# Gated linear attention with a soft mixture of experts on one core: products in the q,k tile, one guard on ScalarE, 8 KB weight places, stores from two engines, and a new order of issue

## The chip, the cores and the metric

The kernel runs on 1 core of one Trainium2 chip. The metric is device time in microseconds (us), the median of several runs; before the change it is 292.26 us (3 runs, 291.92 to 292.39). All data are float32. Engines go by the profile's names: PE is TensorE (PEld its weight loads), DVE VectorE, ACT ScalarE, POOL GpSimd, SP SyncE, whose queue here issues the DMAs.

## The reference

A gated linear recurrence with a complex state is computed for 4 batches x 8 heads, 768 steps, head dimension 48; its outputs are the tokens (3072 x 384) of a soft mixture of 8 experts with 4 slots each.

```python
mag = np.sqrt(a_re * a_re + a_im * a_im)
scale = np.minimum(mag, 0.999) / (mag + 1e-06)
a_re_n, a_im_n = (a_re * scale, a_im * scale)
for t in range(S):
    ar, ai = (a_re_n[:, :, t, :, None], a_im_n[:, :, t, :, None])
    new_re = ar * S_re - ai * S_im
    new_im = ar * S_im + ai * S_re
    kv = np.einsum('bhd,bhe->bhde', k[:, :, t], v[:, :, t])
    S_re, S_im = (new_re + kv, new_im)
    y[:, :, t] = np.einsum('bhd,bhde->bhe', q[:, :, t], S_re)
...
logits = x @ phi
d = softmax of logits over the tokens;  slot_input = d.T @ x
for e in range(E):
    h = np.maximum(slot_input[e] @ w1[e], 0.0)
    slot_out[e] = h @ w2[e]
c = softmax of logits over the slots;   return c @ slot_out
```

## The kernel before, in words

**Tiles.** The 768 steps of a batch are cut into 6 blocks of 128, 24 blocks g in all; three blocks make a unit u (8 units), whose gates, q and k, and v are loaded in one DMA each (tiles `aat`, `qkt`, `vt`, two buffers each). The weights of the experts are cut into chunks in the order in which they are used, 12 chunks of w1 with 8 KB and 11 of w2 with up to 9 KB in each partition. 17 of the 23 fit into places that are free before the experts begin: 7 in the pool `wx`, 4 in the last buffers of `aat` and `qkt`, 4 in `we`, 2 in `wt`. The other 6 reuse `wx` once the hidden layer has read what lies there.

**Steps.** All work is written as small generators, one for each task; a task's name is a letter and a number, and each time that its name stands in the string `ORDER` its next step is issued. `_InOrder` then pins the order on every engine: what stands first in `ORDER` runs first on its engine, and different engines meet only by their semaphores. SP's DMAs are pinned among themselves too, so one that waits holds back those behind it. The steps which matter here:

- `g` (gates, a group of blocks; group 0 is the first block alone, group 1 the rest of unit 0, group 2 is unit 1): a guard (L647 on DVE for the groups below `GUARD_V`, L650 on ACT for the others), then logarithm and exponential on ACT (L652, L654), two steps of DVE (L656, L658), ACT L660, DVE L662, ACT L664, DVE L666. `t` takes the arctangents (L682).
- `e` (exponentials of a block): PE sums the logarithms (`lp`, L724), ACT makes two exponentials into `ee` (L731, L733), and a DMA takes one row of them to `rows` (L736). `d` loads these rows back as the decay of the state (`rt`, L740).
- `p` (phase): DVE carries the phase from the block before (L690), PE sums (`up`, L693), DVE or ACT rounds (L697, L699), DVE L702, ACT the sine (L707), DVE L710, ACT the cosine (L712).
- `m` (products): DVE multiplies q and k by the exponentials, in place in `ee` (L747), then expands the result by sine and cosine into `hat` (L752).
- `x` transposes (PE L764, copy by DVE L768 or ACT L770), `c` scores (PE L775, mask on DVE L779), `a` attends (PE L800 and L802, ACT L805), `D` updates the state (PE L813, DVE L818, L820), `f` turns the output (PE L825).
- `l`, `q`, `s`, `me`, `si` are the router, its running softmax and the merge into the slots' inputs; `er` makes the tokens' weights (PE L290); `H`, `R`, `U`, `X` are the experts (hidden layer L241, then L271, 128 output columns in each of three X), `O` the slots' outputs (L282, L284), `A` combines (PE L300, evicted by ACT L306 or DVE L308) and `S` stores (L981, four stores for each X).
- `wu` are 19 products of a tile of zeros (`blank`, L928) between the first steps of PE; `w` load weights; `i`, `la`, `lq`, `lv` load the inputs; `rp` loads two constant matrices; `L` and `T` load ACT's tables.

The in-place product is the reason why a DMA stands among the computing engines: L747 writes `ee`, from which the row transfer L736 reads, so it waits for that transfer to land.

Of the kernel before, what the change touches and what calls it, by code (L numbers as in the profile page):

```python
# [95 lines left out]
class _Moe:  # L96
# [220 lines left out]
    p4 p4 x6 g3 g3 e4 e4 e4 D1 p4 e4 x8 x10 c3 g3 x8 a0 D1 D2 x10 p5 p5 c4 p5 g3 g3 la2 T2 p3 p3 D1 p3 D2 p5 p5 c3 a1 a1 a1 c5
    m3 c4 p4 p4 p4 D2 D2 c5 wu10 t3 a2 p5 p5 m3 a2 g3 x14 a2 L3 m4 p6 x12 p6 e5 m5 x13 p6 l0 l0 f2 D3 g4 x13 x14 f2 p7 p7 x12 m5
    p7 p7 g4 x15 e6 x15 e6 e6 D3 e8 e8 e8 p8 d1 c6 m4 c6 e6 l0 D3 q0 q0 g4 f0 f0 x19 x17 x17 g4 g4 x19 p8 q0 x16 x16 e7 e7 e7 s0
    c7 c7 x21 x21 g4 m6 x18 x18 f1 f1 a3 tr0 g4 p8 p8 a3 a3 g4 x20 x20 T3 D3 p6 p6 lq2 e7 la3 q0 lv1 c8 c8 c9 D4 D4 g4 x23 p6 s0  # L320
    s0 x22 x22 c10 p8 p8 a4 c9 a4 t4 x23 m6 x27 p8 p9 p7 p7 D4 p7 c10 c11 D4 c11 L4 m7 p9 p9 p9 a4 m7 x25 e8 x25 x24 x24 p10 g5
    rp0 D5 D5 x27 e9 e9 e9 d2 g5 q0 q0 a5 a5 D5 e9 x26 x26 e10 m8 m8 c12 s0 c12 x31 rp1 g5 x28 x31 q0 x28 c13 e10 e10 g5 g5 a5
    p10 p10 p10 x35 w0 c13 x30 x30 l1 g5 l1 x35 x32 p11 e11 e11 e11 x29 x29 x32 g5 g5 q1 q1 q1 a6 a6 e10 a6 m10 f4 f4 c15 p11
    p11 x34 c15 T4 x34 g5 g5 p9 p9 p9 q1 p11 p11 c14 c14 D6 t5 i5 D6 D6 D6 x33 x33 f3 f3 s0 s0 p11 a7 lv2 p11 a7 p10 q1 q1 a7 D7
    m9 p10 D7 m9 D7 e11 m11 p12 c16 p12 p10 p12 l1 c17 c17 D8 x37 x39 D8 la4 g6 c16 a8 a8 m10 L5 x37 g6 d3 lq3 g6 x39 x36 x36 q1
    x41 x41 x38 g5 e13 x40 e13 e13 x38 D7 D8 lv3 c18 x40 e12 e12 a8 D9 e12 e12 g6 s1 x43 x43 p13 g6 e13 m11 g6 c19 c18 c19 g6
    x42 x42 D8 p13 p13 p13 w1 e14 e14 p14 e14 m12 e14 D9 x45 x45 g6 c20 a9 a9 T5 a9 c20 f5 c21 f5 c21 x44 x44 D9 x47 p12 p12 p12
    g6 p14 p14 p14 x47 la5 x46 x46 p13 p13 f7 f7 p14 p14 t6 l2 l2 a10 lq4 a10 m12 c23 s1 g6 p13 D10 f6 f6 p14 p15 p15 s1 p15 c23
    g6 q2 x50 q2 p15 d4 x50 x51 x51 p15 D10 D9 a10 p15 p15 p16 L6 c22 e15 c22 c25 x48 x48 p16 p16 a11 a11 m13 x49 m13 D10 D11
    D11 x53 g7 p16 e15 c25 e15 p17 x49 e16 m14 m14 c24 q2 c24 a11 s1 e17 g7 e16 e16 D11 g7 g7 e17 e17 x55 x55 x53 s1 s1 a12 a12  # L330
    x54 x54 p17 p17 e15 e16 l2 s2 g7 x52 x52 p17 m15 q2 g7 g7 x57 x57 D12 x56 x58 x58 l3 x56 l3 c27 a12 lv4 x59 x59 c27 l3 g7 s2
    s2 c26 q2 f10 D11 q2 w2 f8 w3 c28 c26 a13 a13 T6 t7 f8 p18 m15 f10 p16 p16 p16 D12 p17 p17 q2 f9 p17 g7 p18 c28 x63 f9 s2
    x63 x61 x61 x62 x62 D12 D13 p18 p19 la6 q3 D13 a13 p18 x60 x60 p19 p19 c29 p18 m16 c30 p18 q3 m16 p19 e17 g7 c29 g8 p19 lq5
    L7 x67 q3 a14 a14 s2 x67 f11 f11 d5 a14 lv5 g7 e18 D12 D13 D14 x65 D14 e18 e18 g8 g8 s2 c30 m17 m17 c31 e19 e19 e19 x64 x65
    x64 D13 x68 x68 a15 c31 a15 lq6 s3 x69 e20 e20 x69 g8 e20 g8 p19 g8 x66 x66 p20 e18 m18 s3 s3 m18 c32 c32 x71 T7 s3 p20 D14
    l4 a15 f12 p20 t8 p19 c33 c33 f12 e19 c34 e20 p20 x71 a16 a16 q3 p20 p20 q3 p20 c34 D15 g8 x70 x72 m19 q3 x70 x73 d6 c35 D14
    D15 x72 l4 q4 c35 q3 m19 D15 x73 c36 s3 L8 s3 a16 g8 a17 a17 a17 x76 g8 g8 x78 x78 c36 p21 q4 D16 q4 x75 x75 f13 w4 x76 g8
    l5 w5 l5 e23 e23 x74 D16 x74 x77 f13 m20 m20 x77 p21 p21 p21 e23 c37 x79 e22 e22 e22 c37 x80 q4 x80 e21 e21 e21 f15 e21 x79
    l4 D16 p22 f14 f14 q4 q4 f15 D16 q4 a18 a18 q5 c38 q5 x83 c38 x81 a18 s4 s4 s4 f16 lv6 q5 T8 s4 x83 m21 p22 p22 c39 c39 a19
    a19 x81 p22 p23 p22 p21 p21 e22 p21 m21 s4 s4 p23 p23 p23 f16 x82 x82 p23 p23 D17 D17 D17 D17 c40 c40 x84 c41 c41 x86 D18  # L340
# [4 lines left out]
    er1 w9 w12 ze0 si0 er3 er2 si0 w11 H0 H0 H0 H0 H0 H0 H0 G0 H0 H0 R0 H0 w10 w13 w14 H0 er1 w15 w16 q7 q7 q7 er2 U0 U0 H0 U0
    X0 X0 X0 X0 X0 R1 q7 U1 er7 er7 U1 X0 X0 X0 X0 U1 X0 X0 X0 X0 X0 X0 G0 G0 X0 X1 w17 w18 X1 X1 X1 X1 X1 O0 O0 A3 A4 A5 A5 A2
    A2 A3 X1 X1 X1 A4 S1 S3 X1 X1 X1 X1 A0 A0 er8 A1 er6 X1 X1 X1 X2 X2 A1 X2 X2 X2 X2 O1 er8 O1 S0 er6 A6 A6 S2 A13 A13 A8 A8
    X2 A12 A7 A12 S6 A10 X2 X2 X2 X2 G0 G0 G0 A7 S4 X2 X2 X2 X2 A10 X2 O2 O2 A9 A9 S5 G0 A11 A14 A11 A15 A15 A14 S8 A17 A16 A16
# [197 lines left out]
def _polar(ctx, tc, cst, phi_sb, rp, bad, aa, qk, vv, phi, w1, w2, consts, out):  # L546
# [79 lines left out]
    def wload(pool, **kw):  # L626
# [5 lines left out]
        if x < NW1:  # L632
            SP.dma_start(out=t[:, 0 : W1C * F_], in_=w1[x])
        else:
            c = W2C if x < NW1 + NW2 - 1 else W2L
            SP.dma_start(out=t[:, 0:c], in_=w2[x - NW1][:, 0:c])
# [479 lines left out]
```

## Time and profile before

| what | value |
|---|---|
| runs | 292.39, 291.92, 292.26 us |
| profiled execution | 291.88 us, span 290.1 us |
| granted clock of TensorE, mean | 0.978 |
| busy: PE, PEld | 270.6, 216.3 us |
| busy: DVE, ACT, POOL | 233.2, 218.2, 5.0 us |
| DMA | 54.84 MB, 189 GB/s in the mean |

The span is from the first to the last instruction; the rest of the execution's own time lies around it. A busy time is the time in which the engine executes; a matmul's end is modelled, so a busy PE may also be waiting. Each row of a view by windows gives, for a stretch of the span, the busy time of each engine (with the number of instructions), the clock granted to TensorE as a share of full speed, the share of time in which the DMA engines move data, and GB/s. A row of the chain of waits gives the start, the length, and what was on the chain that ended last. A row of a timeline gives start, length, engine, line, operation, output and inputs, and in brackets how long the engine had been idle and what ended that.

### The profile page before, as it was taken

The page shows a single profiled execution, that of the slowest core. Times are in us where ns is not written, and L with a number is a line of the kernel's source. Part 1 is how long each engine was busy: PE and PEld are TensorE (multiplying, and loading weights), DVE is VectorE, ACT ScalarE, POOL GpSimd, SP SyncE. Part 2 cuts the span into 40 slices and gives each one's busy share as a digit, 9 for nine tenths or more (in the row PEclk, how much of TensorE's full clock was granted, in tenths as well). Part 3 has the DMA queues.
Part 4 walks back from the last instruction along what each step waited for, and adds up shares of the span by engine and source line. Part 5 has one row for each costly group of instructions (what it writes and reads, how often), then busy time and mean ns, then how long its engine had stood idle before and what let it go on. Part 6 is the DMA issues. An engine that isn't in the chain of part 4 may idle for free.

```text
span 290.1 us, 6872 instructions
## 1 busy us (share of the span) xinstructions
PE 270.6 (93%) x2825; PEld 216.3 (75%) x2825; DVE 233.2 (80%) x424; ACT 218.2 (75%) x394; POOL 5.0 (2%) x11
## 2 busy tenths in 40 slices
...
GB/s 251 364 181 2 165 104 27 309 6 29 344 37 21 215 241 90 84 127 336 15 71 397 234 98 150 85 209 2 80 17 384 365 421 422 105 418 419 235 315 186
DMA packets 20054, 54.84 MB, mean 189 GB/s; under 512 B 11632, under 2 KB 12336, under 8 KB 15408
## 3 DMA queue, kind: packets, MB, share of 16 engines
...
## 4 chain that ended last, share of the span: by engine, by line
PE 80%; DMA 6%; DVE 5%; ACT 4%; issue 1%; SPq 1%; ACTq 0%; DVEq 0%
PE sp L775 14%; PE tp L764 14%; PE db L813 8%; PE yb L800 8%; PE yb L802 6%; PE up L693 4%; DMA rows<-ee 4%; PE op L271 4%; PE xp L825 4%; PE hp L241 4%; PE lp L724 3%; PE lg L118 3%; PE sip L185 2%; DMA aat<-in_aa_dram 2%; PE wp L928 1%; PE o L300 1%
## 5 line engine op out<-in xcount | busy, mean ns | idle before, releaser
L764 PE MATMUL tp<-cst,hat 128*96 128x128 f32 x384 | 53.9, 275 | 3.5 <-DVE hat L752 3.4
L770 ACT COPY hT<-tp 96x512 f32<-96x512 f32 x92 | 51.2, 589 | 6.5 <-PE tp L764 4.3
L764 PEld LDWEIGHTS tp<-cst,hat 128*96 128x96 f32 x384 | 42.3, 128 | 12.2 <-issue 8.1
L775 PE MATMUL sp<-hT,hT 96*128 96x128 f32 x384 | 50.5, 277 | 0.0
L775 PEld LDWEIGHTS sp<-hT,hT 96*128 96x128 f32 x384 | 47.3, 192 | 3.5 <-issue 0.6
L752 DVE TENSOR_TENSOR hat<-ee,cs 128x1536 f32<-128x1536 f32 x24 | 42.0, 1752 | 1.2 <-ACT cs L712 0.7
L800 PE MATMUL yb<-scT,vt 128*48 128x128 f32 x384 | 36.2, 276 | 0.0
L779 DVE TENSOR_TENSOR scT<-sp,cst 128x512 f32<-128x512 f32 x48 | 32.6, 684 | 3.6 <-PE sp L775 3.4
L813 PEld LDWEIGHTS db<-vt,hat 128*96 128x96 f32 x320 | 30.8, 165 | 1.8 <-issue 0.9
L802 PE MATMUL yb<-hT,st 96*48 96x128 f32 x320 | 31.2, 272 | 0.0
L813 PE MATMUL db<-vt,hat 128*96 128x48 f32 x320 | 31.2, 244 | 0.0
L800 PEld LDWEIGHTS yb<-scT,vt 128*48 128x48 f32 x384 | 21.1, 122 | 6.2 <-issue 2.6
L747 DVE TENSOR_TENSOR ee<-ee,qkt 128x768 f32<-128x768 f32 x24 | 22.6, 950 | 2.5 <-DMA rows<-ee 2.4
L928 PE MATMUL wp<-blank 128*128 128x512 f32 x38 | 21.9, 708 | 1.0 <-POOL blank L923 1.0
L693 PE MATMUL up<-aat,cst 128*128 128x384 f32 x48 | 20.1, 500 | 0.0
L802 PEld LDWEIGHTS yb<-hT,st 96*48 96x48 f32 x320 | 19.2, 123 | 0.0
L805 ACT COPY yT<-yb 128x512 f32<-128x512 f32 x24 | 14.3, 594 | 5.7 <-PE yb L802 5.7
L712 ACT ACTIVATE cs<-n,kb 128x384 f32<-128x384 f32 x24 | 14.7, 612 | 2.0 <-DVE n L710 2.0
L731 ACT ACTIVATE ee<-lp 128x384 f32<-128x384 f32 x24 | 12.1, 505 | 5.2 <-PE lp L724 3.6
L928 PEld LDWEIGHTS wp<-blank 128*128 128x128 f32 x38 | 8.6, 238 | 9.3 <-issue 6.5
L724 PE MATMUL lp<-aat,cst 128*128 128x384 f32 x24 | 11.0, 541 | 4.4 <-DVE aat L666 4.4
L707 ACT ACTIVATE cs<-f 128x384 f32<-128x384 f32 x24 | 12.5, 525 | 2.6 <-DVE f L702 2.5
...
## 6 DMA issues: line engine op xcount, KB each, us to landing
...
```

Source lines behind the costliest of these rows:

```text
L693: PE.matmul(out=up, lhsT=tri_u[par], rhs=ph, start=True, stop=True)
L724: PE.matmul(out=lp, lhsT=mask[par], rhs=aat[u][:, j, 0], start=True, stop=True)
L747: DVE.tensor_tensor(out=e, in0=e, in1=qkt[u][:, j], op=ALU.mult)
L752: DVE.tensor_tensor(out=x, in0=e.rearrange("p w (h d) -> p w h d", d=D).unsqueeze(3).broadcast_to(sh), in1=cs[g].unsqueeze(1).broadcast_to ...
L764: PE.transpose(out=tp[:, a, :], in_=hat[g][w][:, 4 * hh + a].rearrange("p c d -> p (c d)"), identity=ident)
L770: ACT.copy(out=hT[g, hh, w], in_=tp)
L775: PE.matmul(out=sp[:, a, :], lhsT=hT[g, hh, 1][:, a, :], rhs=hT[g, hh, 0][:, a, :], start=True, stop=True)
L779: DVE.tensor_tensor(out=t, in0=sp, in1=mask[g % 2].unsqueeze(1).broadcast_to([P, 4, P]), op=ALU.mult)
L800: PE.matmul(out=o, lhsT=vt[u][:, j, h, :], rhs=scT[g, hh][:, a, :], start=True, stop=first)
L802: PE.matmul(out=o, lhsT=st[g - 1][:, h, :], rhs=hT[g, hh, 0][:, a, :], start=False, stop=True)
L813: PE.matmul(out=db[:, h, :], lhsT=hat[g][1][:, h].rearrange("p c d -> p (c d)"), rhs=vt[u][:, j, h, :], start=True, stop=True)
L928: PE.matmul(out=wp.rearrange("p (a c) -> p a c", a=4), lhsT=blank, rhs=blank.unsqueeze(1).broadcast_to([P, 4, P]), start=True, stop=True)
```

## The change

- `mults` writes the products of q, k and the exponentials into the q,k tile and no longer into `ee`; the expansion reads them there.
- `GUARD_V` goes from 3 to 2: the guard of group 2 (unit 1) is done by ACT (L650) and no longer by DVE (L647).
- The places of weights are 8 KB (`W2C` 2048 where it was 2304), w2 has 12 chunks, and `wx` has 8 places, `we` 5: 19 of 24 chunks have a place ahead and 5 reuse `wx`. The output tiles keep their width under a name of its own (`OSC`).
- The row transfer of the first block, and every second store, are issued by ACT.
- `blank` lies in a buffer of `xs`, which it gives back.
- `ORDER` is new in all its lines.

```diff
-W1C, W2C = 2, 2304
+W1C, W2C = 2, 2048
+OSC = 2304
...
-NW1, NW2 = 12, 11
-W2L = 64 * HD - (NW2 - 1) * W2C
-BUF = dict(wx=7, wt=2, f=3, cs=4, ee=3, hat=2, hT0=4, hT1=3, scT=2, st=2, xs=5, yT=5, we=4)
+NW1, NW2 = 12, 12
+BUF = dict(wx=8, wt=2, f=3, cs=4, ee=3, hat=2, hT0=4, hT1=3, scT=2, st=2, xs=5, yT=5, we=5)
...
-SPLIT, GUARD_V, ROUND_V, COPY_V = 4, 3, 4, 1
+SPLIT, GUARD_V, ROUND_V, COPY_V = 4, 2, 4, 1
...
-        SP.dma_start(out=rows[u][:, j, :]...)
+        (SP if g else ACT).dma_start(out=rows[u][:, j, :]...)
...
-        e = ee[g]
-        DVE.tensor_tensor(out=e, in0=e, in1=qkt[u][:, j], op=ALU.mult)
+        qk = qkt[u][:, j]
+        DVE.tensor_tensor(out=qk, in0=ee[g], in1=qk, op=ALU.mult)
...
-            in0=e.rearrange("p w (h d) -> p w h d", d=D).unsqueeze(3).broadcast_to(sh),
+            in0=qk.rearrange("p w (h d) -> p w h d", d=D).unsqueeze(3).broadcast_to(sh),
...
-    blank = cp.tile([P, P], F32, name="blank")
+    blank = ys.tile([P, HD], F32, name="xs", bufs=BUF["xs"])[:, 0:P]
...
-        SP.dma_start(out=stored(out, x, s), in_=os_at(x, *STORES[s]))
+        (ACT if s % 2 else SP).dma_start(out=stored(out, x, s), in_=os_at(x, *STORES[s]))
```

Of the order, the head (to about the first score), some places of the middle, and the end of the merge and of the stores, before and after; steps left out stand as "...":

```diff
-    wu2 i0 g0 wu3 wu18 L0 g0 g0 i2 g0 g0 g0 i4 i3 g1 g0 g0 g1 g0 wu16 wu4 g1 g1 i1 e0 wu15 e0 e0 i6 T0 t0 lq0 g1 t1 wu6 p0 wu5
-    p0 p0 wu13 p0 i7 p0 p0 L1 e0 m0 wu9 g1 m0 x3 g1 wu8 g1 p1 x3 wu14 g1 e1 la0 e1 rp1 g2 g2 g2 x2 x2 e1 e1 p1 p1 wu7 x0 e2 e2
-    e2 p1 p2 g2 g2 g2 m1 x0 p2 T1 p1 wu0 x1 wu12 t2 D0 x1 p2 wu17 p1 wu11 p2 la1 p1 p2 e2 d0 wu1 g2 rp0 c0 lv0 p2 p3 m1 D0 p2 m2
-    L2 c1 x5 g2 g2 x4 x4 x5 c0 p3 p3 g3 g3 e5 ...
+    wu6 wu4 wu1 L0 wu12 wu18 i0 g0 g0 g0 g0 g0 wu17 i3 g0 g0 wu5 g0 i4 g1 g1 g1 rp1 i1 g0 e0 e0 e0 wu3 wu9 T0 t0 g1 g1 t1 e0 i2
+    m0 p0 p0 p0 p0 p0 p0 L1 p1 g1 p1 m0 g1 i7 g1 wu16 i6 wu2 p1 p1 g1 p2 rp0 D0 x2 x2 p2 p2 x3 x3 p2 la0 g2 g2 g2 g2 g2 e1 e1 e1
+    wu0 x1 x1 e2 e2 e2 x0 g2 T1 p1 wu14 lv0 wu10 p2 t2 D0 x0 c0 g2 c0 la1 p1 p1 p2 p2 wu15 m1 a0 p3 wu7 L2 m1 c1 c1 p3 p3 g2 g2
+    x4 x4 a0 a0 x5 x5 wu13 m2 p3 e1 e2 g3 e3 ...
...
-    ... la5 x46 x46 p13 p13 f7 f7 p14 p14 t6 l2 l2 a10 lq4 a10 m12 c23 s1 g6 ... x53 g7
+    ... p14 t6 x46 x46 g6 p12 p12 D9 ... f7 l2 a10 a10 a10 m12 w2 f6 f6 c22 c22 p15 q2 p15 x47 x47 p14 p14 la5 g7
...
-    q7 f20 q7 f20 w7 w8 f23 er0 me0 er0 s6 me0 s6 f21 f21 f22 me0 s7 er4 me0 s7 s7 er3 me0 me0 me0 me0 f22 s7 s7 er5 er5 q7 er4
-    er1 w9 w12 ze0 si0 er3 er2 si0 w11 H0 H0 ...
+    f20 f20 q7 f23 f23 q7 s7 me0 me0 s6 s6 f22 i5 s6 f21 s7 s7 f22 s7 er1 me0 f21 s7 me0 me0 me0 me0 er0 s7 ze0 q7 q7 w13 w12
+    w11 er4 me0 er1 si0 si0 H0 H0 ... U0 er2 er2 U1 w14 er8 U1 er6 ... X0 er5 er3 ... er7 er3 ...
...
-    X2 A12 A7 A12 S6 A10 ... X2 O2 O2 A9 A9 S5 G0 A11 A14 A11 A15 A15 A14 S8 A17 A16 A16
-    A18 A18 A19 A17 S9 A19 A20 S11 A20 S10 S7
+    ... X2 S4 X2 X2 S5 O2 O2 A13 A13 A12 A14 A15 A12 S6 A14 A18 A15 S8 G0 A18 A11 A11 S7 A16
+    A16 A19 A19 S11 A17 A17 S9 A20 A20 S10
```

More of the change, by code (lines that the diff above doesn't have):

```diff
@@ L317 @@
[L317 to L340, printed above, removed]
@@ L345 @@
[L345 to L348, printed above, removed]
@@ new lines @@
+    g3 g3 x7 g3 x7 D1 p4 D1 p5 e4 lq0 g3 x8 x8 wu11 m3 p5 e4 e4 p5 p5 D2 c3 g3 D2 c5 c3 T2 e3 rp1 t3 p3 p3 p3 a1 a1 p6 D1 la2 p5
+    p5 g3 e6 c5 p4 p5 p4 c4 m3 x12 lq1 x13 e4 D2 c4 a1 p6 m4 D3 D3 a2 p6 a2 m5 p7 p4 m4 x12 x13 D2 c6 x14 g4 c6 L3 a2 D3 l0 l0
+    l0 g4 w0 e5 e6 g4 g4 e6 x14 x16 x16 x19 x19 D4 e8 x18 e8 e8 x15 x15 p7 x18 p7 g4 g4 x17 a3 x17 m5 s0 p7 p8 e7 f0 f0 g4 q0 q0
+    e6 e7 e7 d1 D3 g4 f2 f2 c7 c7 c8 c8 p8 la3 q0 q0 s0 T3 p8 x20 lv1 m6 t4 lq2 p8 p7 a3 p7 p7 a3 x21 D4 p6 p6 c9 p8 x23 p9 e7
@@ new lines @@
+    s0 c9 p9 p6 x20 q0 a4 a4 x21 tr0 g4 m6 q0 x23 x22 x22 q0 rp0 p8 p9 c10 w1 c10 p8 D4 x27 x27 a4 g5 L4 x26 x26 s0 x25 x25 e8
+    g5 c11 x24 x24 p9 D5 D5 g5 e9 m8 e9 e9 c11 e10 e10 d2 D4 a5 a5 m7 f1 f1 e10 lv2 m7 x31 x31 x28 x28 c13 m8 p10 p10 g5 g5 p10
+    a5 c12 x30 p10 x29 c12 g5 e11 x29 l1 a6 x30 c13 p11 l1 a6 g5 e11 e11 m11 c14 lq3 D5 q1 q1 x34 a6 g5 c14 x34 p11 p11 m9 q1 q1
+    c15 c15 T4 t5 f3 x33 p9 p10 la4 f3 D6 D6 x35 x35 p11 s0 p9 p9 D6 D6 p12 l1 p11 p11 x32 p10 s0 m9 x32 f4 f4 g5 p11 p10 a7 a7
@@ new lines @@
+    p15 g6 x50 x50 p15 p15 p15 e14 D10 D10 lq4 d4 x51 p16 D10 c23 c23 L6 w3 x48 x51 q2 x49 m13 e15 e15 e15 x48 e15 g7 m14 m14
+    a11 a11 c25 c25 p16 D11 p16 p16 D11 g7 g7 x49 p17 e16 e16 e16 x55 x57 x55 a11 e17 g7 e17 c24 e17 D11 c24 x57 l2 x54 x54 x56
+    D11 p17 p17 l3 p17 g7 g7 q2 q2 l3 x52 x52 s1 x53 a12 a12 x53 x56 s1 lv4 c27 c27 la6 s1 s2 c26 c26 m15 g7 x58 x59 f8 c28 a12
+    e16 a13 a13 T6 p17 p17 t7 x59 p18 p16 D12 g7 p17 p16 x58 c29 p18 a13 w4 m15 q2 D12 p16 f8 m17 x61 w5 p18 s2 c29 g8 c28 p19
@@ L478, in chunk @@
             t = wk.tile([P, W2C], F32, name="sw", bufs=6)
-            n = W1C * F_ if w is w1 else W2C if x < NW2 - 1 else W2L
-            ACT.dma_start(out=t[:, 0:n], in_=w[x][:, 0:n])
+            ACT.dma_start(out=t, in_=w[x])
             chunk.n += 1
```

36 lines of the change are left out of this document (24 added, 12 removed).

## The prediction

> **What bounds the kernel now.** I read the busy time by stretch first, with the cuts at places of the chain, then the chain of waits, then timelines of the first 20 us and the last 12.
>
> ```profile
> 19.49:41.20 21.71, 18.36 (x82) 11.15 (x82) 20.55 (x27) 15.27 (x21) 0.95 (x1) 0.92 0.40 114
> 41.20:60.00 18.80, 18.75 (x183) 15.76 (x184) 18.37 (x28) 18.68 (x31) 0.77 (x2) 1.00 0.48 137
> 60.00:180.00 120.00, 120.00 (x1258) 105.71 (x1257) 115.83 (x185) 118.70 (x216) 0.00 (x0) 1.00 0.52 151
> 180.00:250.00 70.00, 69.51 (x765) 59.74 (x762) 55.76 (x123) 46.64 (x97) 2.03 (x3) 1.00 0.57 214
> 250.00:278.30 28.30, 27.26 (x511) 17.01 (x511) 11.20 (x38) 5.53 (x12) 0.49 (x1) 1.00 0.77 307
> 278.30:290.10 11.80, 2.74 (x9) 1.30 (x9) 2.66 (x5) 2.82 (x6) 0.00 (x0) 0.75 0.62 243
> ```
>
> Columns: stretch, length, busy time of PE, PE's weight loads, DVE, ACT, POOL, granted clock, DMA share, GB/s. From 19.49 to 41.20 DVE works 20.55 of 21.71 us and ACT only 15.27: DVE bounds the head. From 41 to 180 all three are full (ACT 118.70 of 120). After 180 ACT and DVE have room and PE runs on; after 250 it is nearly alone. So what the head saves can reach the end, if the middle doesn't eat it.
>
> ```profile
> 8.12 0.96 DVE gt L647 x2
> 9.08 0.59 DVE aat L662
> ...
> 10.95 1.57 PE lp L724 x2
> ...
> 13.06 5.29 DMA rows<-ee
> 18.42 0.97 DVE ee L747
> ...
> 39.79 1.37 DVE aat L666
> 41.20 0.91 PE lp L724 x2
> 42.12 0.89 PE sp L775 x8
> 43.01 1.01 PE yb L800 x16
> ```
>
> This is the chain (start, length, what). Three places matter. At 8.12 DVE does the guard of the second gate group, after waiting for its load, before the first block's L662. At 13.06 the one-row transfer out of `ee` goes out, lands 5.29 us later, and only then the in-place product L747 starts. At 39.79 the gates of unit 1 are done, and PE gets the sums that it waited for; from here on it has no gap to speak of.
>
> **The head, step by step.** ACT's rows:
>
> ```profile
> 7.06 0.61 ACT L660 ACTIVATE gt<-gt,kb 128x384 f32<-128x384 f32 x1 [1.23 <-DVE tmax L658]
> ...
> 10.21 0.83 ACT L652 ACTIVATE aat<-aat 128x768 f32<-128x768 f32 x1
> 11.07 0.84 ACT L654 ACTIVATE gt<-aat 128x768 f32<-128x768 f32 x1
> ...
> 13.43 1.28 ACT L584 ACT_TABLE_LOAD   x1
> 14.73 1.25 ACT L682 ACTIVATE aat<-aat 128x384 f32<-128x384 f32 x2
> 17.43 0.52 ACT L707 ACTIVATE cs<-f 128x384 f32<-128x384 f32 x1 [1.45 <-DVE f L702]
> 17.86 0.60 ACT L712 ACTIVATE cs<-n,kb 128x384 f32<-128x384 f32 x1
> ```
>
> (a) The new order puts L662 ahead of the guard. It can start when L660 ends, 7.67, and ends at about 8.3; the guard then runs to 9.3 (its data no longer lies behind a q,k piece in the queue), L666, of L662's length, to 9.9, where the matmul starts: 1.0 us earlier than 10.95. ACT puts the second group's logarithm and exponential (0.83 and 0.84) between 9.3 and 11.0, beside the matmul's 1.57, then the two exponentials of L731 and L733, which here took the 0.9 us from the matmul's end at 12.52 to the table load at 13.43; I get 12.0 for their end, 13.3 for the arctangents against 14.73. From the arctangents to the sine it took 2.70 us (PE, then DVE twice), so the sine starts at 16.0 and the cosine ends at 17.1.
>
> (b) The products go into the q,k tile, so L747 waits for no row to land. It now stands before the rounding, at about 13.1, under the phase matmul. The expansion L752 then waits for the cosine alone: 17.1 against 19.49, with which the first stretch above begins: 2.4 us earlier. The row transfer is issued by ACT behind the arctangents, and holds ACT less than the 1.45 us for which it waited there anyway; if it holds it longer than that, the sine is late by the rest.
>
> (c) From that expansion to the end of unit 1's gates DVE decides. The list of its steps in both orders differs by this: the guard of unit 1 and one product leave (the product comes later), two masked scores enter.
>
> ```profile
> 24.44 1.35 DVE L647 TENSOR_SCALAR_CACHE_REDUCE gt<-aat 128x1152 f32<-128x1152 f32 x1
> ```
>
> ```profile
> L779 DVE TENSOR_TENSOR scT<-sp,cst 128x512 f32<-128x512 f32 x48 | 32.6, 684 | 3.6 <-PE sp L775 3.4
> ...
> L290 PE MATMUL ep<-ecT,rp 96*128 96x512 f32 (+2 forms) x18 | 4.5, 351 | 0.0
> ```
>
> That is -1.35 - 0.97 + 2 x 0.68 = -1.0 us of work. Against it I count 0.5 us of waits that were not there (mostly DVE waiting for the logarithm while ACT does the guard that it took over: 1.25 us, if it runs at L652's pace, 0.83 for two thirds of the width). So the gates of unit 1 end 2.4 + 1.0 - 0.5 = 2.9 us earlier. What DVE and ACT have left at that point is the same to 0.5 us in both orders, and PE has done the first block's attention more, which here comes after 41.20 (L800, 1.01). Bounds: 1.5 (ACT's guard on the path in full) to 3.9 (PE's 1.0 carried as well). I take 2.9, the number of DVE, which bounds this stretch.
>
> **The middle.** The rest of the order is mixed anew, but steps of PE stand, all along, behind nearly the same sums of DVE's and ACT's work as before; I price that at nothing, with 2 us either way. ACT covers it: if its 118.70 of 120 rises, there is nothing to take it up until 180.
>
> ```profile
> DVE ee L747 <- DMA rows<-ee: 2.4, 3, 1.1
> ...
> PE op L271 <- issue: 1.0, 1, 1.0
> ...
> PE lg L118 <- DVE d L176: 0.5, 1, 0.5
> ```
>
> These rows (waiting engine, what for; us, times, longest) show three waits of L747 on a row, 2.4 us of DVE; the head's is one, so two of at most 1.1 lie elsewhere. I see one of them reach PE, as the 0.5 us before L118. With the product in the other tile they are gone: 0.5 us, between 0 and 2.2. In exchange the q,k tile comes free an expansion later, so the next load of q,k and what stands behind it on SP's queue (the row transfers, the decay loads, and the state scaling that waits for these) could be late. In the new order each such load stands well behind the expansion that frees it, so I take nothing.
>
> **The tail.** The weights:
>
> ```profile
> 254.00:270.00 16.00, 15.11 (x288) 9.17 (x280) 4.94 (x12) 3.48 (x8) 0.00 (x0) 1.00 1.00 414
> ```
>
> From 254 to 270 all DMA engines move the last six chunks, 414 GB/s x 16 us = 6.6 MB, and PE's wait of 1.0 us above, with no other releaser, lies at the end of that. With 8 KB places 19 of 24 chunks fit ahead instead of 17 of 23, and five are left, 5 x 1.05 = 5.2 MB, 12.7 us: the 1.0 us goes. But three wide weight tiles (L290: nine in 4.5 us, so 0.5 each) move from before the hidden layer to after it, where PE has no gap; ahead of it they filled a wait of the merge, which gets shorter by part of that. I take 0.5 us for both together, between -0.5 and 1.5.
>
> ```profile
> 268.80 16.41 SPq L981 DMA_DIRECT2D out_dram<-os  x12
> ```
>
> ```profile
> 281.99 3.22 SPq L981 DMA_DIRECT2D out_dram<-os  x3
> ```
>
> The twelve stores are issued by SP one behind the other, and the last three alone take 3.22 us, of the 11.80 after the last expert product. With two issuers none stands behind another for so long, but ACT issues three between its last evictions, which at 3.22/3 can delay one of them by up to 1.1 us each. I take 0.5 us, from -1.0 to 1.5. The Trainium skill, "DMA: Bandwidth & Descriptors", section "Issuing engines are not separate DMA queues", says that issuing from several engines saves only the sequencer's time, as all run on the same 16 engines; by that the bytes still set the end and the sum would be 0.5 us smaller. No row here shows a store issued by ACT.
>
> Sum: 2.9 + 0.5 + 0.5 + 0.5 = 4.4 us. The profiled execution took 291.88 us, span 290.1, so 287.5 after; the median of the runs is 292.26, 0.4 above it, so I forecast 287.9.
>
> **The rivals.** *The middle eats the head's gain* (0.15). ACT at 118.70 of 120 is the engine that bounds from 60 to 180 and a new order costs it what the head brought: then 2.9 and the 0.5 are lost, 292.3 - 1.0 = 291.3. For it: PE's weight loads are busy for only 105.71 of 120, so PE's 120.00 may hide waiting. Against it: ACT had 6 us idle in the second stretch, where the guard goes, and 23 after 180. The Trainium skill, "Perfetto Trace Analysis", section "Identifying the Most-Contended Engine", holds matmul busy time for a bad measure and weight-load time for a good one; by that ACT is the bound here, and this rival the likelier.
>
> *Slower: a load of the gates comes too late* (0.10). In the new order the load for unit 6 stands one step ahead of its first use, the guard on ACT, and right behind a weight chunk on SP's queue; before there was no chunk there and some 60 steps between. SP runs ahead, to where the buffer comes free, some 40 steps earlier, 16 of them ACT's: at the third stretch's 118.70 us for 216 instructions, 8.8 us. A transfer behind two large loads landed after 5.29 us above, and these two are 2.2 MB, again 5.3 us at 414 GB/s. It decides from 9 us on. If the landing takes 14, ACT, which is full there, stands 5 us for it, and as its place is bare the whole kernel does; like loads follow for unit 7 and for q,k. That gives 292.3 - 4.4 + 5 = 292.9, and more if the second stops too.
>
> *More comes through* (0.13). PE's 1.0 us of extra work counts, the upper ends of the two tail terms hold (1.0 each), and 0.7 more of L747's waits: 287.9 - 3.7 = 284.2.
>
> *The change doesn't do what it says*: a row transfer issued by ACT could hold ACT's own stream long enough to undo (b); that costs 1 us and lies in the range.
>
> **How the numbers follow.** The forecast has 0.62, and its own range is 285.5 to 290.0 (2 us of the middle, the ends of the tail terms). The range reaches from the case of more to the case of the eaten gain: 284.2 to 291.5; the slower case and a little at each end stay outside. What a measurement of this kernel can tell is about 0.2%, 0.6 us. Faster: forecast, more, and 0.10 of the 0.15 of the eaten gain, 0.85; same 0.05; slower 0.10.
>
> **What would show it.** In the profile after: no "DVE <- DMA rows" wait at L747's line; the first expansion near 17 us and the gates of unit 1 ending near 38; DVE as full as now between them; the window from 60 to 180 as full on ACT; the expert products without the 1.0 us gap, DMA done some 3 us sooner; the last store issued within 5 us of the last expert product. I am wrong if PE or ACT shows waits of over 1 us between 60 and 240, if ACT's first sine starts later than 16.5, or if the evictions on ACT stand behind its stores.

## The result, and the profile after

The kernel after takes 288.2 us (median of 4 runs, 288.19 to 288.68) against 292.09 us (4 runs): ratio 0.988, 95% interval 0.9846 to 0.9914. The profiled execution took 288.19 us, span 286.4, mean clock 0.98. The forecast was 287.9 us, so the time came out as predicted; its terms did not all do so, and some of its reasons were wrong.

In the profile after, line numbers are five lower: the product is L742, the expansion L747, the guard L642 (DVE) or L645 (ACT), the last step of the gates L661, the sine L702, a row transfer L731, the decay load L735, the state scaling L815, a store L976. In kernels made from the one before, they are one lower (L746, L751, L646 or L649, L665).

The span falls into five stages, cut at the end of the gates of unit 1, the end of the last logits, the first product of the hidden layer, and the end of the last expert product (all from the timelines). The lengths in us:

| kernel | first expansion | gates of unit 1 end | to last logits | merge | experts | end | span |
|---|---|---|---|---|---|---|---|
| before | 19.49 | 41.15 | 200.5 | 8.4 | 28.2 | 11.9 | 290.1 |
| after | 16.81 | 38.12 | 201.0 | 7.8 | 27.7 | 11.9 | 286.4 |
| difference | -2.7 | -3.0 | +0.5 | -0.6 | -0.5 | 0.0 | -3.7 |

By windows, with these cuts (stretch, length, busy time of PE, PE's weight loads, DVE, ACT, POOL, then granted clock, DMA share, GB/s):

```profile
16.81:38.12 21.31, 20.50 (x98) 12.18 (x98) 19.38 (x26) 17.93 (x23) 0.00 (x0) 0.87 0.22 62
38.12:60.00 21.88, 21.88 (x197) 18.22 (x197) 21.38 (x30) 21.78 (x37) 0.00 (x0) 1.00 0.59 212
60.00:180.00 120.00, 119.54 (x1251) 104.30 (x1253) 115.39 (x184) 116.47 (x211) 0.00 (x0) 1.00 0.49 158
180.00:246.89 66.89, 66.43 (x747) 57.75 (x738) 51.93 (x122) 45.60 (x97) 2.52 (x3) 1.00 0.58 217
246.89:274.55 27.66, 27.66 (x514) 17.84 (x514) 11.45 (x37) 5.15 (x11) 0.00 (x0) 1.00 0.66 263
274.55:286.40 11.85, 2.71 (x10) 1.49 (x10) 3.17 (x6) 2.88 (x6) 0.00 (x0) 0.81 0.61 240
```

Two rows speak against the forecast. In the first, DVE works 19.38 of 21.31 us, less fully than the 20.55 of 21.71 before, where it was to be the bound. In the third, ACT has fallen from 118.70 to 116.47: the middle is less full, not as full. The experts' row has no gap left (27.66 of 27.66).

The head in the timeline after (start, length, engine, line, operation, output and inputs, in brackets the idle time before and its cause):

```profile
9.91 0.91 PE L719 MATMUL lp<-aat,cst 128*128 128x384 f32 x2 [0.48 <-DVE aat L661]
...
12.81 0.95 DVE L742 TENSOR_TENSOR qkt<-ee,qkt 128x768 f32<-128x768 f32 x1
12.93 1.23 ACTq L731 DMA_DIRECT2D rows<-ee  x1
...
15.75 0.52 ACT L702 ACTIVATE cs<-f 128x384 f32<-128x384 f32 x1 [1.45 <-DVE f L697]
...
16.81 1.76 DVE L747 TENSOR_TENSOR hat<-qkt,cs 128x1536 f32<-128x1536 f32 x1
...
22.01 1.26 ACT L645 ACTIVATE gt<-aat,kb 128x1152 f32<-128x1152 f32 x1 [1.03 <-DVE aat L661]
...
36.76 1.36 DVE L661 SCALAR_TENSOR_TENSOR aat<-aat,gt 128x1152 f32<-128x1152 f32 x1
```

The first sum starts at 9.91 (forecast 9.9), the product waits for no row, ACT's row transfer takes 1.23 us of its queue and leaves the sine's wait at the same 1.45 us, the expansion starts at 16.81 (forecast 17.1), and unit 1's gates end at 38.12 (forecast about 38.2).

The middle has a wait that was not there before. The waits between 127 and 167 us (waiting engine, what for; us, times, longest):

```profile
DVE st L815 <- PE lp L722: 1.6, 1, 1.6
ACT n L694 <- PE up L688: 1.5, 4, 0.5
```

PE's `lp` had long been done when DVE went on; the chain shows the real cause (start, length, what):

```profile
125.14 0.35 SPq L591
125.49 0.04 issue
125.53 7.48 DMA rows<-ee
133.02 0.02 issue
133.03 0.33 SPq L735
133.36 0.04 issue
133.40 3.48 DMA rt<-rows
...
137.00 0.55 DVE st L815
```

The row transfer of block 14 goes out behind the load of the gates for unit 6 (L591) and needs 7.48 us; SP holds the decay load back until it has landed, and the state scaling waits for that, 1.65 us. PE, which has no other wait of more than 0.2 us in the stage to the last logits, stands still for 0.27 us of it:

```profile
138.21 0.42 PE L795 MATMUL yb<-scT,vt 128*48 128x128 f32 x4 [0.27 <-DVE scT L774]
```

The end of the chain:

```profile
277.37 0.70 DVE os L308
278.07 0.34 ACTq L976
278.41 0.05 issue
278.46 0.49 ACT os L306
```

ACT's last eviction stands behind the issue of a store, which the forecast had named as a sign of being wrong. The last store goes out 4.4 us after the last expert product, as forecast (within 5), yet the end still lasts 11.85 us.

### The profile page after: what moved, and what is told of

Read it like the earlier page. It is cut to its first block, busy times and chain, and to the rows that moved or that the text cites. A ratio compares the mean times of both kernels' runs of the same rounds, so it can differ in the third digit from the quotient of the medians.

```text
span 286.4 us, 6873 instructions
## 1 busy us (share of the span) xinstructions
PE 270.8 (95%) x2825; PEld 216.5 (76%) x2825; DVE 232.0 (81%) x422; ACT 219.5 (77%) x396; POOL 4.3 (2%) x11
## 4 chain that ended last, share of the span: by engine, by line
PE 78%; DVE 5%; ACT 4%; DMA 4%; issue 1%; SPq 0%; ACTq 0%; DVEq 0%
PE sp L770 14%; PE tp L759 13%; PE yb L795 8%; PE db L808 7%; PE yb L797 6%; PE up L688 5%; PE op L271 4%; PE hp L241 4%; PE xp L820 4%; DMA rows<-ee 3%; PE lg L118 2%; PE lp L719 2%; PE sip L185 2%; PE lp L722 1%; PE o L300 1%; DMA rt<-rows 1%
## 5 line engine op out<-in xcount | busy, mean ns | idle before, releaser
L759 PE MATMUL tp<-cst,hat 128*96 128x128 f32 x384 | 53.2, 274 | 0.6 <-DVE hat L747 0.6
L747 DVE TENSOR_TENSOR hat<-qkt,cs 128x1536 f32<-128x1536 f32 x24 | 41.9, 1751 | 0.5
L795 PE MATMUL yb<-scT,vt 128*48 128x128 f32 x384 | 36.4, 277 | 0.3 <-DVE scT L774 0.3
L808 PEld LDWEIGHTS db<-vt,hat 128*96 128x96 f32 x320 | 31.6, 167 | 3.1 <-issue 1.9
L808 PE MATMUL db<-vt,hat 128*96 128x48 f32 x320 | 31.9, 246 | 0.0
L795 PEld LDWEIGHTS yb<-scT,vt 128*48 128x48 f32 x384 | 20.8, 122 | 6.2 <-issue 2.3
L688 PE MATMUL up<-aat,cst 128*128 128x384 f32 x48 | 21.0, 519 | 3.3 <-DVE aat L685 2.2
L923 PE MATMUL wp<-xs 128*128 128x512 f32 x38 | 22.1, 708 | 1.0 <-POOL xs L918 1.0
L742 DVE TENSOR_TENSOR qkt<-ee,qkt 128x768 f32<-128x768 f32 x24 | 22.8, 949 | 0.0
L800 ACT COPY yT<-yb 128x512 f32<-128x512 f32 x24 | 14.1, 586 | 10.3 <-PE yb L797 10.1
L923 PEld LDWEIGHTS wp<-xs 128*128 128x128 f32 x38 | 8.1, 227 | 8.8 <-issue 5.9
L697 DVE SCALAR_TENSOR_TENSOR f<-n,up 128x384 f32<-128x384 f32 x24 | 13.2, 548 | 1.9 <-ACT n L694 1.5
L820 PE MATMUL xp<-cst,yT 128*128 128x128 f32 x96 | 14.2, 276 | 0.0
L726 ACT ACTIVATE ee<-lp 128x384 f32<-128x384 f32 x24 | 11.9, 494 | 2.8 <-PE lp L722 2.4
```

The lines of the kernel that those rows point to most:

```text
L688: PE.matmul(out=up, lhsT=tri_u[par], rhs=ph, start=True, stop=True)
L742: DVE.tensor_tensor(out=qk, in0=ee[g], in1=qk, op=ALU.mult)
L747: DVE.tensor_tensor(out=x, in0=qk.rearrange("p w (h d) -> p w h d", d=D).unsqueeze(3).broadcast_to(sh), in1=cs[g].unsqueeze(1).broadcast_t ...
L759: PE.transpose(out=tp[:, a, :], in_=hat[g][w][:, 4 * hh + a].rearrange("p c d -> p (c d)"), identity=ident)
L795: PE.matmul(out=o, lhsT=vt[u][:, j, h, :], rhs=scT[g, hh][:, a, :], start=True, stop=first)
L808: PE.matmul(out=db[:, h, :], lhsT=hat[g][1][:, h].rearrange("p c d -> p (c d)"), rhs=vt[u][:, j, h, :], start=True, stop=True)
```

## Experiments

The theory that I started from is the forecast's: each part acts where it stands, the head's lead passes through the middle, and the middle's loss is the late decay load. The rival: the new mix of ACT's and PE's work costs the middle, and the head's lead is worth less. Each time below is a median; the kernel before took 291.6 to 291.9 us beside these runs. The kernel after was not run again beside them; its 288.2 us comes from the measurement above, in which the kernel before took 292.09, so that a difference of less than 0.5 us from it is not decided by these medians.

**Products in the q,k tile alone, old order.**

```diff
-        e = ee[g]
-        DVE.tensor_tensor(out=e, in0=e, in1=qkt[u][:, j], op=ALU.mult)
+        e = qkt[u][:, j]
+        DVE.tensor_tensor(out=e, in0=ee[g], in1=e, op=ALU.mult)
```

> The kernel before, in its own order, with one edit: the products of q, k and the exponentials go into the q,k tile and no longer into ee. Theory 1: no product waits for a row; the first expansion starts when the cosine ends, 18.5 instead of 19.49, DVE passes that 1.0 us on, and the two waits in the middle (1.1 us at most each, one of which PE shows at about 173 to 182) give up to 1.1 more: 1.0 to 2.1 us faster, 290.0 to 291.1. Theory 2 (the middle is bound by ACT and takes what the head brings): 292.1 within 0.5 us.

289.44 us, ratio 0.9926 (0.9897 to 0.9955): 2.2 us, a little over the upper end of theory 1. In its timeline the expansion starts when the cosine ends:

```profile
17.46 0.60 ACT L711 ACTIVATE cs<-n,kb 128x384 f32<-128x384 f32 x1
18.37 1.76 DVE L751 TENSOR_TENSOR hat<-qkt,cs 128x1536 f32<-128x1536 f32 x1
```

The gates of unit 1 end 1.4 us earlier (39.74), and the stage from there to the last logits takes 199.9 us instead of 200.5: L747's two waits in the middle were worth 0.6 us, and PE's wait of 0.5 us before the logits, on which the forecast had put them, is gone.

**The second group's guard behind L662 as well, old order.**

```diff
-    ... i4 i3 g1 g0 g0 g1 g0 wu16 ...
+    ... i4 i3 g0 g0 g1 g1 g0 wu16 ...
```

> The kernel before with the products in the q,k tile, and one step of the order moved: the guard of the second gate group goes behind the first group's L662 on DVE. Theory 1: the first sum on PE starts 1.0 us earlier, and without the row's landing that goes on to the cosine and the first expansion: 1.0 us faster than with the products alone, 2.0 to 3.1 us faster than the kernel before. Theory 2: DVE is the bound behind the first expansion and the guard is still to be done by it, so that the second group is later by as much as the first is earlier: no faster than with the products alone.

288.63 us, ratio 0.9903 (0.9873 to 0.9932): 3.0 us faster than the kernel before, the upper end of theory 1. Two small edits in the old order give all but 0.4 us of what the whole change gives. Its head:

```profile
16.96 1.76 DVE L751 TENSOR_TENSOR hat<-qkt,cs 128x1536 f32<-128x1536 f32 x1
...
22.22 1.35 DVE L646 TENSOR_SCALAR_CACHE_REDUCE gt<-aat 128x1152 f32<-128x1152 f32 x1
...
36.98 1.36 DVE L665 SCALAR_TENSOR_TENSOR aat<-aat,gt 128x1152 f32<-128x1152 f32 x1 [0.17 <-ACT gt L663]
```

The gates end at 38.34 with the guard still on DVE, 0.2 us behind the kernel after. The lead at the gates, 2.8 us, is 3.4 us at the last logits: the middle takes nothing of it.

The granted clock differs from run to run, and the runs of the kernel before are shorter where it is higher: over all its runs beside these experiments the median is 292.0 us at a mean clock of 0.976 to 0.981 and 291.1 at 0.986 to 0.992. That is not the gain: at 0.986 to 0.992 the medians are 289.2 us with the products alone (3 runs) and 288.5 with both edits (4).

**The guard of unit 1 on ACT too, old order.**

```diff
-SPLIT, GUARD_V, ROUND_V, COPY_V = 4, 3, 4, 1
+SPLIT, GUARD_V, ROUND_V, COPY_V = 4, 2, 4, 1
```

> The kernel before with the products in the q,k tile, the second group's guard behind L662, and the guard of unit 1 on ACT (GUARD_V = 2): every edit of the head, in the old order. Theory 1 (DVE's sum bounds the head, as forecast): 1.35 us less on DVE and 0.5 us of waits, so unit 1's gates end 0.85 us earlier than with the guard on DVE, 37.5 instead of 38.34, and the time is 287.8. Theory 2 (the chain through the gates of unit 1 bounds it: the guard starts when L661 of the group before is done, at 22.22 on DVE and at 22.01 on ACT, and takes 1.35 or 1.26 us): 0.0 to 0.3 us earlier, 288.3 to 288.6.

290.18 us, ratio 0.9938 (0.9914 to 0.9962): 1.6 us slower than with the guard on DVE. Both theories missed.

```profile
23.59 0.49 ACT L730 ACTIVATE ee<-lp 128x384 f32<-128x384 f32 x1 [2.32 <-PE lp L723]
23.98 1.25 ACT L649 ACTIVATE gt<-aat,kb 128x1152 f32<-128x1152 f32 x1
...
38.70 1.41 DVE L665 SCALAR_TENSOR_TENSOR aat<-aat,gt 128x1152 f32<-128x1152 f32 x1 [0.17 <-ACT gt L663]
```

On ACT's queue the guard stands behind an exponential that waits 2.32 us for PE's sum, and starts at 23.98 instead of 22.22. The windows from 17 to 38.3, of this kernel and then of the one with the guard on DVE:

```profile
17.00:38.30 21.30, 16.20 (x78) 9.68 (x78) 17.94 (x24) 16.11 (x21) 0.04 (x1) 1.00 0.32 92
```

```profile
17.00:38.30 21.30, 17.02 (x82) 10.27 (x82) 20.56 (x27) 15.99 (x20) 0.69 (x1) 1.00 0.39 108
```

DVE has the guard's 1.35 us less to do, stands idle 3.4 of 21.3 us instead of 0.7, and the gates end 1.8 us later (40.11), of which 0.4 were lost by the first expansion (17.36). DVE's sum is therefore not the bound.

**The guard of unit 1 back on DVE, new order.** The diff is the reverse of the last one, applied to the kernel after.

> The kernel after, with the guard of unit 1 on DVE again (GUARD_V = 3). Theory 1 (DVE bounds the head and the middle passes the lead on): 1.35 us more on DVE between the first expansion and the end of unit 1's gates, less the 0.5 us for which DVE waited on ACT's guard: 0.9 us slower, 289.1. Theory 2 (ACT bounds the middle, and the head's lead is worth nothing there): ACT has 1.26 us less to do, and the time stays at 288.2 or falls a little.

293.56 us, 5.4 us slower than the kernel after, ratio to before 1.0049 (1.0025 to 1.0072). Neither theory has that. A part of it goes with the clock: its three runs with a mean clock of 0.976 to 0.981 took 292.0 to 292.4 us, the six at 0.965 took 293.5 to 294.0. The first three are still 3.9 us slower in the median than the kernel after, whose runs had 0.979 to 0.986.

```profile
25.52 1.34 DVE L642 TENSOR_SCALAR_CACHE_REDUCE gt<-aat 128x1152 f32<-128x1152 f32 x1
...
41.91 1.35 DVE L661 SCALAR_TENSOR_TENSOR aat<-aat,gt 128x1152 f32<-128x1152 f32 x1
```

In the new order five steps of DVE stand between L661 and the guard's place, so it starts at 25.52 instead of 22.01. From the start of the guard to the end of unit 1's gates it takes 16.1 us in the kernel after, in the old order with the products alone (23.62 to 39.74), with two edits (22.22 to 38.34) and with ACT's guard (23.98 to 40.11). It takes 16.7 in the kernel before (24.44 to 41.15), where ACT's logarithm stands behind an exponential that waits for PE's sum, and 17.7 here, where the granted clock between 17 and 38 us was 0.74, PE's steps are longer, and DVE comes to the last step 1.7 us after ACT has its input ready. This chain, alternating between DVE and ACT, bounds the head where PE does not hold it up; what counts is when the guard starts.

**Products in place again, new order.**

```diff
-        qk = qkt[u][:, j]
-        DVE.tensor_tensor(out=qk, in0=ee[g], in1=qk, op=ALU.mult)
+        qk = ee[g]
+        DVE.tensor_tensor(out=qk, in0=qk, in1=qkt[u][:, j], op=ALU.mult)
```

The first block's product stands behind its phase, and the expansion reads `ee`. In the new order some row transfers stand behind the product of their block; they then carry products in place of decays, and the kernel's own flag makes it compute everything a second time by a slow path. Its total, 7788.72 us, says nothing of the edit; the head does.

> The kernel after, with the products in place in ee again, and the first block's product behind its phase, as it stood before. Theory 1: the product waits for the row that goes out at 12.93 and needs some 5.3 us, so it starts at 18.3, ends at 19.2, and the first expansion starts 2.4 us later than at 16.81; DVE passes it on to the end of unit 1's gates; with 0.5 us more for products behind late rows in the middle the kernel takes 2.9 us longer, 291.1. Theory 2: the middle takes the head's lead anyway, the row was not what counted: under 1 us slower.

```profile
18.34 0.96 DVE L742 TENSOR_TENSOR ee<-ee,qkt 128x768 f32<-128x768 f32 x1 [1.54 <-DMA rows<-ee]
19.41 1.76 DVE L747 TENSOR_TENSOR hat<-ee,cs 128x1536 f32<-128x1536 f32 x1
```

The product starts at 18.34 (18.3 expected) and the expansion 2.6 us later than in the kernel after. Its last gate step ends at 40.12, 2.0 us later. That is theory 1 for the head; its total for the kernel is not testable here.

**The row of block 14 ahead of the loads.**

```diff
-... m12 w2 f6 ... la5 g7 p15 g6 ... p15 e14 D10 D10 lq4 d4 x51 ... L6 w3 ...
+... m12 e14 w2 f6 ... la5 g7 p15 g6 ... p15 D10 D10 lq4 d4 x51 ... L6 w3 ...
```

> The kernel after, with one step of the order moved: the row transfer of block 14 goes ahead of the weight chunk and of the gates' load for unit 6, behind which it stood on SP's queue. Theory 1 (late decay load): in the kernel after this row goes out at 125.53 and lands 7.48 us later, the decay load for unit 4 waits for it on SP and lands 3.48 us after that, and DVE's state scaling stands 1.65 us for it, at a place where ACT and DVE are full; by that the time falls by 1.6 us, to 286.6, the wait of DVE at L815 is gone, and the middle costs nothing against the kernel before. Theory 2 (the mix): the 1.8 us that the kernel after loses between 128 and 166 us come from how the new order mixes the work of ACT and PE, and the wait of DVE is only where it shows; then the time stays at 288.2 within 0.3 us.

291.78 us, ratio 1.001 (0.9984 to 1.0035): 3.6 us slower than the kernel after, against both theories. The waits between 110 and 170 us, and the piece of the chain:

```profile
DVE st L815 <- PE lp L722: 4.5, 1, 4.5
ACT gt L645 <- DMA aat<-in_aa_dram: 2.8, 1, 2.8
```

```profile
125.09 11.39 DMA aat<-in_aa_dram
```

The load of the gates for unit 6 went out as before but needed 11.39 us, and ACT stood 2.8 us for it. The stage to the last logits takes 204.2 us.

**Further, the next weight chunk behind the row of block 15.**

```diff
-... L6 w3 x48 ... e15 e15 e15 x48 e15 g7 ...
+... L6 x48 ... e15 e15 e15 x48 e15 w3 g7 ...
```

> The kernel after, with the row transfer of block 14 ahead of the weight chunk (as in the run with that step alone) and, further, the next weight chunk on SP's queue put behind the row transfer of block 15, where it cannot share the engines with the gates' load for unit 6. In the run with the first step alone the decay load was issued at 127.92 instead of 133.03, but with it the weight chunk at 129.34 instead of 134.23, and the gates' load then took 11.39 us to land and ACT waited 2.8 us for it: 3.6 us slower. Theory 1 (two queue effects, each with its own price): with the chunk out of the way the gates' load lands in time, the state scaling at L815 finds its decay, and the time falls by 1.6 us, to 286.6. Theory 2 (the order's mix costs the middle, whatever the queue does): 288.2 within 0.3 us.

291.33 us, ratio 0.9991 (0.9961 to 1.0021): the chunk was not the cause; the load still needs 11.69 us. The windows show when the loads move, first here, then in the kernel after:

```profile
124.00:126.00 2.00, 2.00 (x19) 1.56 (x16) 2.00 (x4) 1.99 (x5) 0.00 (x0) 1.00 0.13 21
126.00:127.00 1.00, 1.00 (x13) 0.83 (x14) 0.97 (x4) 1.00 (x2) 0.00 (x0) 1.00 0.23 49
127.00:128.00 1.00, 1.00 (x26) 0.80 (x28) 0.90 (x3) 1.00 (x3) 0.00 (x0) 1.00 1.11 74
128.00:129.00 1.00, 1.00 (x20) 1.00 (x22) 0.97 (x3) 1.00 (x2) 0.00 (x0) 1.00 0.71 82
```

```profile
124.00:126.00 2.00, 2.00 (x20) 1.49 (x16) 2.00 (x3) 1.99 (x5) 0.00 (x0) 1.00 0.45 106
126.00:127.00 1.00, 1.00 (x13) 0.83 (x11) 0.97 (x4) 1.00 (x2) 0.00 (x0) 1.00 0.87 328
127.00:128.00 1.00, 1.00 (x26) 0.80 (x26) 0.90 (x2) 1.00 (x3) 0.00 (x0) 1.00 1.35 392
```

The weight chunk was issued at 122.08 behind the row, the gates' load at 125.05, and until 129 the rate stays at 82 GB/s or less, whatever is moved; between 127 and 128 the DMA engines are full at 74 GB/s. In the kernel after, where the chunk stands ahead of this row (121.48), the loads run at over 300 GB/s from 126.

**The row of block 14 issued by ACT**, its step moved in the order to right behind the exponentials that it carries.

```diff
-        (SP if g else ACT).dma_start(out=rows[u]...)
+        (ACT if g in (0, 14) else SP).dma_start(out=rows[u]...)
```

> The kernel after, with the row transfer of block 14 issued by ACT, right behind the exponentials that it carries (about 121), so that it stands on another queue than the loads; SP's loads keep their order and lose nothing but this row. In the two runs with this row ahead of the loads on SP's own queue, the weight chunk issued behind it at 122.1 moved almost nothing until 129 (21 to 82 GB/s between 124 and 129, where the kernel after moved 106 to 392), and the gates' load landed at 136.5. Theory 1 (the middle's loss is the late decay load; on one queue a row transfer holds up the loads behind it, on two it doesn't): the decay is there in time, the 1.65 us wait at L815 goes, ACT, which is full there, pays 0.7 to 1.2 us for the issue: 287.5 to 287.9, and the gates' load lands before ACT needs it at 133.7. Theory 2 (the mix of the order costs the middle): nothing is gained and ACT pays for the issue: 288.9 to 289.4. Theory 3 (rows and loads disturb one another whoever issues them): ACT waits for the gates' load again, 291.

289.46 us, ratio 0.9913 (0.988 to 0.9945): 1.3 us slower than the kernel after (the profiled run, 288.89 us, is one of its faster ones). That is close to theory 2's number (288.9 to 289.4), but says nothing for its cause, since DVE's wait at L815 is still there, 2.1 us. The chain:

```profile
121.13 5.24 DMA rows<-ee
...
126.88 10.66 DMA rt<-rows
```

The decay load goes out 6.5 us earlier and lands at 137.5 all the same (136.9 in the kernel after): it stands on SP's queue behind three loads of 1.0 to 1.2 MB. So theory 1's remedy fails for a third reason. The loads hold up the decay. And with the row on ACT's queue the loads reach 319 GB/s only from 128 us, where the kernel after has 328 from 126: a row seems to hold up loads on another queue as well. That is read from the windows of these runs; how it comes about is not shown.

**All stores by SP.**

```diff
-        (ACT if s % 2 else SP).dma_start(out=stored(out, x, s), in_=os_at(x, *STORES[s]))
+        SP.dma_start(out=stored(out, x, s), in_=os_at(x, *STORES[s]))
```

> The kernel after, with all twelve stores issued by SP again. Theory 1 (issuing counts, as forecast): the stores stand one behind another on SP, 0.5 us slower, 288.7. Theory 2 (bytes): from the last expert product, 274.59, the DMA engines move 2.8 MB at about 390 GB/s until 282.3 whoever issues it, and the span ends 11.8 us after that product in both kernels; then nothing changes, 288.2 within 0.3 us. Theory 3: two of the last evictions on ACT stand behind a store's issue (0.34 us each, one of them on the chain); without them 0.3 to 0.7 us faster.

288.17 us, ratio 0.9863 (0.9823 to 0.9903): theory 2, no difference. The end lasts 11.5 us instead of 11.9, which would agree with theory 3's 0.34 us on the chain, but the medians do not show it, and the last version below, with two issuers and the same 0.34 us on its chain, ends in 11.5 us too.

**The old places of the weights**, in the new order, with the steps of the loads renumbered to fit.

```diff
-W1C, W2C = 2, 2048
+W1C, W2C = 2, 2304
-NW1, NW2 = 12, 12
+NW1, NW2 = 12, 11
-BUF = dict(wx=8, ..., we=5)
+BUF = dict(wx=7, ..., we=4)
```

> The kernel after with the weights' places as before: w2 in 11 chunks of up to 9 KB, 7 places in wx and 4 in we, so 17 of 23 chunks are loaded ahead and six chunks reuse wx. Theory 1: six reloads are 6.6 MB, 16 us instead of 12.7, the expert products wait 1.0 us for the last of them as in the kernel before, and the stores start behind them: 1.0 us slower, 289.2. Theory 2: the expert products reach the last chunk later in the new order (three wide weight tiles lie ahead of them), so that the wait is covered: within 0.3 us of 288.2.

288.78 us, ratio 0.9902 (0.9874 to 0.993). The median is 0.6 us above the kernel after, between the two theories, and no stage of its trace shows where. For the weights the trace decides for theory 2: the experts take 27.7 us as in the kernel after, with no gap. The reloads do take longer,

```profile
264.00:266.00 2.00, 2.00 (x53) 1.58 (x52) 1.36 (x3) 0.37 (x1) 0.00 (x0) 1.00 1.02 412
```

to about 267 instead of 263 us, but products out of the last chunks start only after that.

**The first third's combining and stores earlier.**

```diff
-... A4 w17 A4 A1 A1 G0 A0 X1 w18 er7 X1 X1 X1 X1 X1 A0 A5 S3 A5 A6 A6 S2 A2 S0 A2 A3 A3 X1 X1 X1 O1 O1 ... S1 ...
+... A4 w17 A4 A1 A1 S3 X1 A0 w18 er7 A0 S0 A5 X1 A5 A6 A6 S2 A2 X1 A2 A3 A3 S1 X1 X1 G0 X1 X1 X1 X1 O1 O1 ...
```

> The kernel after with the combining of the first 128 output columns and its four stores moved ahead in the order, right behind its expert products; nothing else is changed. Theory 1 (bytes set the end): the DMA engines do next to nothing from 263 to 270 us (share 0.02 to 0.19) and then move stores at 390 GB/s until 282.3; with the first stores some 3 us earlier about 0.9 MB less is left at the last expert product, and the end comes about 2 us earlier, 286.2. Theory 2 (the chain of evictions and issues sets the end): the last store is issued at 278.98 as before, and the time stays at 288.2 within 0.3 us.

288.97 us, ratio 0.9907 (0.988 to 0.9935): no gain, and inconclusive on what sets the end. The first stores do go out earlier, but the experts take 28.5 us, 0.8 more, and towards their end the DMA engines have little to move (the kernel after moves 395 GB/s there):

```profile
272.00:274.60 2.60, 2.60 (x69) 2.15 (x62) 1.49 (x4) 1.09 (x2) 0.00 (x0) 1.00 0.39 146
```

After the last expert product there are 2.8 MB left, as in the kernel after (each a sum of GB/s by time), and the end again lasts 11.8 us.

**A version out of the parts that helped.** The old order, with the two edits of the head (guard of unit 1 on DVE, first row by SP), to the last logits; from there the new order, with the 8 KB places and both issuers of stores.

```diff
-    wu6 wu4 wu1 L0 wu12 wu18 i0 g0 g0 g0 g0 g0 wu17 i3 g0 g0 wu5 g0 i4 g1 ...
+    wu2 i0 g0 wu3 wu18 L0 g0 g0 i2 g0 g0 g0 i4 i3 g0 g0 g1 g1 g0 wu16 ...
...
     l7 l7 l7 f19 f19 q7 q7 s6 s6 f20 ...
```

> The old order to the last logits, with the products in the q,k tile and the second group's guard behind L662 (guard of unit 1 on DVE, first row by SP), and from there the new order with the 8 KB places and the stores from two engines. Theory 1 (the parts add): the last logits end at 238.2 as in the old order with the two edits, 0.9 us ahead of the kernel after, whose queue stops its middle; the merge takes 7.8 us as in the kernel after instead of 8.4, the experts 27.7 instead of 28.1, the end 11.8: span 285.5, 287.4, 0.8 us faster than the kernel after. Theory 2: the new tail owes its times to what the new middle left done ahead of it; then the merge takes 8.4 us again and the kernel 288.0 to 288.6.

287.25 us (287.09 to 287.86), ratio 0.9842 (0.9801 to 0.9884): theory 1, 0.15 us from its number, and no run of it is as long as the shortest of the kernel after. The stages add up: gates end 38.48, then 199.9, 7.8, 27.7 and 11.5 us.

```profile
60.00:180.00 120.00, 120.00 (x1261) 105.63 (x1256) 116.77 (x188) 118.67 (x216) 0.00 (x0) 1.00 0.52 150
```

ACT is as full as before the change, and the head's lead comes through.

## Why the prediction came out

That the total came so near is in part luck: the span fell by 3.7 us, where the terms gave 4.4, and within that the head came out 0.1 us better, the tail 0.6 better, the middle 1.0 worse and the stores 0.5 worse than forecast.

**The head** was to bring 2.9 us and brought 3.0. Parts (a) and (b), forecast at 2.4 us to the first expansion, brought 2.7. They hold, and the old order shows them one by one: the gates end 1.4 us earlier with the products and 1.4 more with the guard moved. Part (c) brought 0.35 us for the forecast 0.5 (21.66 us from the first expansion to the gates before, 21.31 after), a nearly right sum from a wrong reason. It took DVE for the bound and priced the guard on ACT at 1.35 us less 0.5 of waits. The chain from the guard's start bounds, and the guard starts at 22.01 on ACT in the new order and at 22.22 on DVE in the old: 0.2 us. Where its place in the queue does not fit, either engine costs more than that: 1.6 us on ACT in the old order, 5.4 on DVE in the new one (3.9 in the runs with a clock like the kernel after's). A busy share of 95% was read as a bound; with 1.35 us less work on DVE the stage ended later.

**The middle** was to bring 0.5 us and cost 0.5. The step that failed is the one that priced the new mix of the order and the loads behind q,k at nothing. L747's waits went as said (0.6 us in the old order, 0.5 forecast). But the stage to the last logits is 201.0 us in the new order and 199.9 in the old one with the same product: 1.1 us lost. The forecast named the queues behind q,k, and dismissed them because each load stood behind the expansion that frees it; it did not look at what stood behind the load. The late decay load that came of it is on the chain, but it explains only a part: PE is idle for 0.5 us of this stage, 0.27 of them there, against 0.1 us in the old order. The other 0.7 us are busy time of PE, 200.47 us against 199.81 in the last version above. The forecast counted the first block's attention, which PE has done ahead of this stage (L795: 35.2 us left instead of 36.2). It did not count the products of zeros (`wu`): the new order puts two of them, and the rest of a third, behind the gates of unit 1, where the old one has one (2.30 us instead of 1.02), and that takes the attention's lead back. PE's other steps differ by up to 0.6 us each, in both directions. Since a busy PE may hide waiting, the share of each cause is not shown, and no run moved the products of zeros. Which order of SP's queue would lift DVE's wait is open: after three attempts it was 2.1 to 4.7 us. A weight chunk moved out of the stretch ahead of the gates' load was not tried.

**The slower rival** did not happen in the kernel after, but its mechanism is real. It decided from a landing time of 9 us on, with ACT standing for the rest. With landings of 11.39 and 11.69 us ACT stood 2.8 and 3.1 us: the point is 8.6 us. **The eaten gain** did not happen either: ACT at 118.7 of 120 passes a lead on in full. A stage that is full takes up nothing, but it gives nothing back; this is how I read it, and no run tells it from a bound by PE, whose 120.00 of 120 is as full. The 6 us of idle ACT that the forecast held against this rival belong to the first stretch of its table (15.27 of 21.71), not the second. By the Trainium skill, "Perfetto Trace Analysis", section "Identifying the Most-Contended Engine", ACT was the bound there; the traces agree that PE's weight loads had room (105.6 of 120), and that was no reason for this rival.

**The signs** were not all sharp. Waits of ACT of over 1 us between 60 and 240 were to mean that the forecast was wrong; the kernel after has them, up to 4.1 us at L800, but so had the kernel before, up to 3.2, so this sign could not tell. That the window from 60 to 180 is as full on ACT and the head as full on DVE did not come true.

**The tail** was to bring 0.5 us for weights and merge and brought 1.1, inside its bounds. Its reason, five reloads instead of six, is wrong: with six the expert products have no gap either. The order covers them, with other work ahead of the last chunks, and the new tail behind the old middle keeps both 7.8 and 27.7 us. That the moved weight tiles are this work is argued, not shown alone.

**The stores** were to bring 0.5 us and brought none, by any of the views. The Trainium skill, "DMA: Bandwidth & Descriptors", section "Issuing engines are not separate DMA queues", says that issuing from several engines saves only the sequencer's time; the run with all stores on SP agrees, 288.17 against 288.2 us.
